# Attention and a bilinear GLU on one core: in the value products, the order of a head group's pieces

## Chip, core and metric

The kernel runs on one core of one Trainium2 chip. The metric is device time in microseconds (us) for one execution. Before the change it is 262.96 us, the median of 3 runs (262.53 to 263.45).

## The reference

One input x of 2048 rows and 512 columns is normalised and feeds two branches, and x and both branches are added. All tensors are bfloat16.

```
B, S, D = 1, 2048, 512;  H = 32; Dh = 16; W = 256;  F = 1792
xn = _layernorm(x)                                  # no scale, no shift
# branch A: attention in a sliding window
q, k, v = heads of (xn @ wqkv)                      # 32 heads of 16
scores = einsum("bhqd,bhkd->bhqk", q, k) * Dh**-0.5
mask = (i - j >= 0) & (i - j < W)                   # i: query, j: key
p = softmax(where(mask, scores, -1e9))
A = (einsum("bhqk,bhkd->bhqd", p, v), heads side by side) @ wo
# branch B: a GLU whose gate has no nonlinearity
g = xn @ w_gate;  u = xn @ w_up
Bout = (g * u) @ w_down
return x + A + Bout
```

## The kernel before

**Chunks and head groups.** The 2048 rows are worked in 4 chunks T of 512 queries. The 32 heads are handled as 4 head groups c of 8 heads: 128 of the 512 columns of q, which lie on the partitions as 4 row blocks of 32, each with an even and an odd head. A key tile is 128 columns of K: 64 keys for the even head and the same 64 for the odd one (two masks on K, line 284). In a chunk there are 8 such key tiles of its own (m = 0 to 7), and 4 of the chunk before are still inside the window (m = -4 to -1).

**Pieces.** With queries counted in blocks of 64, key tile m meets only its own block and the four behind it. A piece is (m, q0, q1): key tile m against query blocks q0 to q1. The constant `LATER` (line 21) lists the pieces of a head group of chunks 1 to 3 in five batches:

```
LATER = (((-2, 0, 2), (0, 0, 4)), ((5, 5, 7), (1, 1, 5)), ((-3, 0, 1), (7, 7, 7), (3, 3, 7)),
         ((-4, 0, 0), (6, 6, 7), (2, 2, 6)), ((-1, 0, 3), (4, 4, 7)))
```

In columns (64 per query block) that is 192, 320 | 192, 320 | 128, 64, 320 | 64, 128, 320 | 256, 256. A batch fills at most 512 columns, one PSUM bank for each of the four row blocks.

**Scores.** `scores` (line 361) multiplies a batch's pieces for the four row blocks (32x128 array tiles), and ScalarE (ACT) takes the exponential of all of it into a strip P (line 352). GpSimd (POOL) zeroes the far corner of the window (lines 181 and 354), VectorE (DVE) the near one (`mask_diag`, line 439). `strip` (line 325) notes each piece of a batch in `self.parts[T, c]`, in the order in which the strips are made.

**Value products.** `values` (line 451) is called once for each chunk and head group when its strips are masked. It goes through the noted pieces. For each piece there are 8 weight loads and 8 products, on 8 array tiles of 64 rows by 32 columns: two halves of the key tile (`par`: even and odd heads) and four row blocks (`e`). The weights are 32 columns of V, or of VS, which is V with its 64-row halves swapped; the moving operand is the piece's columns of P; the result is added in two PSUM banks `acc` (in the very last call `L`). The value tile carries columns of ones, so the softmax's sums come along. `start` is set on the first piece, `stop` on the last. Two transposes on VectorE (line 476) take the banks out; `divide` (line 480) divides and transposes once more. A head group of chunks 1 to 3 has 12 pieces, so 96 weight loads and 96 products; in chunk 0 it has 9 pieces.

**The order of all work is written out by hand.** `run` (line 630) goes through the batches as steps; between two steps it puts `fillers`: the projections, gate and up products (lines 499 and 510), each 128x512, on PE. `PAIRS` (line 27) says which head groups' values are taken in one go: in chunk 1 and 2 groups 0 and 1, then 2 and 3; in chunk 3 groups 0 and 1, then 2 alone, and 3 alone at the end. So chunks 1 to 3 have seven calls or pairs of calls, and chunk 0 four single ones.

**The down phase.** In chunks 1 to 3 seven batches, from the fourth of head group 0 to the last of head group 1, are taken in `down_phase` (line 398) together with the down products (line 532) of the chunk before. Three of them (the third, fourth and fifth of head group 1) are spread by row block over four steps, and their strips are made before those of the two batches in front of them. So in head group 1 the pieces are noted as 128, 64, 320 | 64, 128, 320 | 256, 256 | 192, 320 | 192, 320; in groups 0, 2 and 3 they stand as in `LATER`.

**Waits.** PE's instructions carry their semaphore waits themselves. The first product of a piece whose columns were masked waits for that mask.

Of the kernel before, what the change touches and what calls it, by code (L numbers as in the profile page):

```python
# [20 lines left out]
LATER = (((-2, 0, 2), (0, 0, 4)), ((5, 5, 7), (1, 1, 5)), ((-3, 0, 1), (7, 7, 7), (3, 3, 7)),  # L21
         ((-4, 0, 0), (6, 6, 7), (2, 2, 6)), ((-1, 0, 3), (4, 4, 7)))
REST = (((0, *SIX), (1, *SIX), (0, *FOUR)), ((1, *FOUR), (2, *FOUR)), ((2, *SIX), (3, *SIX), (3, *FOUR)))
SCORES, VALUES, SECOND = 1.9, 6.0, 5.0
FIRST = 3
GAP = 10.6
# [9 lines left out]
class Kernel:  # L36
# [279 lines left out]
    def batches(self, T):  # L316

        out = []
        for c in range(4):
            out += [tuple((c, *p) for p in pieces) for pieces in (LATER if T else SHARED)]  # L320
            if T == 0 and c < 3:
                out.append(REST[c])
        return out
# [127 lines left out]
    def values(self, T, c, accs=None):  # L451


        nc = self.nc
        if accs is None:
            accs = [self.m_tile([128, 512], F32, "acc") for _ in range(2)]
        todo = self.parts.pop((T, c))
        for i, (P, col, m, q, n) in enumerate(todo):
            U, j = divmod(8 * T + m, 8)
            b, h = divmod(j, 2)  # L460
            for par in range(2):
                rows = slice(64 * par, 64 * par + 64)
                for e in range(4):
                    if par == h:
                        at = 18 * (16 * (2 * b + par) + 4 * c + e)
                        v = self.V[U][rows, at:at + 32]
                    else:
                        at = 18 * (16 * b + 4 * c + e)
                        v = self.VS[U][rows, at:at + 32]
                    nc.tensor.matmul(accs[par][32 * e:32 * e + 32, q:q + n], lhsT=v,  # L470
                                     rhs=P[rows, e, col:col + n], start=(i == 0), stop=(i == len(todo) - 1),
                                     tile_position=(64 * par, 32 * e), skip_group_check=True)

        at = self.work.tile([128, 2, 16, 32], F32, tag="at", name="at")
        for par in range(2):
            nc.vector.transpose(out=at[:, par].rearrange("p b r -> p (b r)"), in_=accs[par][:])  # L476
        self.book("dve", TURN)
        self.at[(T, c)] = at
# [324 lines left out]
```

## Time and profile before

| | |
|---|---|
| median of 3 runs | 262.96 us (262.53 to 263.45) |
| the profiled execution | 262.99 us, its span 261.2 us |
| TensorE (PE) busy | 255.2 us, 98% of the span |
| ScalarE (ACT) busy | 183.4 us, 70% |
| VectorE (DVE) busy | 168.3 us, 64% |
| GpSimd (POOL) busy | 115.2 us, 44% |
| granted TensorE clock | 1.00 in every slice |

The span runs from the first to the last instruction of the program; the time holds what lies around it too (1.8 us here). "PE" are products, "PEld" weight loads, which overlap with them. In the profile's lines, a group of instructions has a line of the kernel, an engine, an operation and its operands with shapes; "xN" counts instructions. The line 470 holds the value products of all calls. The ends of products are modelled in such profiles, so a start is a better witness than an end. Times inside the span count from its start.

### The profile page before, as it was taken

What the parts mean: (1) busy time and instruction counts of PE and PEld (TensorE: products, weight loads), DVE (VectorE), ACT (ScalarE), POOL (GpSimd) and SP (SyncE); (2) the same over time, 40 slices, a digit from 0 to 9 for tenths busy, and PEclk for the clock granted to TensorE, in tenths of its full rate; (3) what the DMA queues carried; (4) which work ended last, traced back from release to release, by engine and by line L of the source; (5) the groups of instructions that cost most, each with busy time, mean ns of one, the idle gap of its engine ahead of it and who ended that gap; (6) DMA issues with size and microseconds to landing.
All of it is one profiled execution on the core that took longest, in us unless ns stands there. A gap on an engine that the chain in (4) does not pass through costs nothing.

```text
span 261.2 us, 7759 instructions
## 1 busy us (share of the span) xinstructions
PE 255.2 (98%) x3154; PEld 119.9 (46%) x3170; DVE 168.3 (64%) x342; ACT 183.4 (70%) x167; POOL 115.2 (44%) x278
## 2 busy tenths in 40 slices
PE   8999999999999999999999999999999999999995
PEld 7434444444444544444544454444544445434453
DVE  6777898888835488347976468641895235948144
ACT  3477778888586788787756768879874877877500
POOL 6226242425356745343445764334242565543500
PEclk9999999999999999999999999999999999999999
DMA  6999910120013230002001300000200100000002
GB/s 203 377 352 340 282 26 20 24 48 1 3 40 43 60 25 1 3 0 48 3 3 41 82 24 23 0 4 1 50 3 5 35 23 24 3 0 3 3 0 83
DMA packets 19426, 15.04 MB, mean 58 GB/s; under 512 B 7360, under 2 KB 19392, under 8 KB 19392
## 3 DMA queue, kind: packets, MB, share of 16 engines
q1 hardware_dynamic: 18848, 14.26, 19.8%
q8 instruction: 26, 0.43, 0.7%
q10 hardware_dynamic: 544, 0.30, 0.4%
q14 instruction: 8, 0.07, 0.1%
HBM read 9.70 MB, written 2.10 MB: 45 GB/s over the span
## 4 chain that ended last, share of the span: by engine, by line
PE 87%; DVE 8%; issue 2%; ACT 1%; DMA 1%; ACTq 1%
PE up L510 17%; PE gp L499 17%; PE psd L532 15%; PE qkp L274 9%; PE S L349 7%; PE acc L470 6%; PE vp L262 5%; PE psd L538 5%; PE L L532 2%; DVE at L476 2%; DVE hT L515 1%; DVE on L489 1%; PE B L349 1%; DMA x<-in_A_x_dram 1%; DVE st L192 1%
## 5 line engine op out<-in xcount | busy, mean ns | idle before, releaser
L181 POOL TENSOR_SCALAR_AFFINE_SELECT P<-P 64x256 bf16<-64x256 bf16 x224 | 99.2, 443 | 122.5 <-ACT P L352 108.0
L352 ACT ACTIVATE P<-S 128x2048 bf16<-128x2048 f32 x66 | 123.8, 1876 | 24.6 <-PE S L349 19.3
L499 PE MATMUL gp<-xnT,Wg 128*128 128x512 bf16 x224 | 59.1, 380 | 0.0
L510 PE MATMUL up<-xnT,Wu 128*128 128x512 bf16 x224 | 59.0, 380 | 0.0
L515 DVE TENSOR_TENSOR hT<-up,gsb 128x512 bf16<-128x512 f32 x56 | 37.9, 683 | 25.4 <-ACT gsb L253 13.1
L532 PE MATMUL psd<-Wd,hT 128*128 128x512 bf16 (+1 forms) x200 | 46.7, 368 | 0.8 <-issue 0.5
L447 DVE TENSOR_TENSOR P<-P,diag 128x512 bf16<-128x512 bf16 (+1 forms) x75 | 29.4, 392 | 16.0 <-ACT P L352 15.9
L253 ACT ACTIVATE gsb<-gp 128x512 bf16<-128x512 f32 x49 | 28.5, 596 | 9.6 <-PE gp L499 9.6
L532 PEld LDWEIGHTS <-hT 128*128 128x128 bf16 x238 | 21.6, 98 | 25.6 <-issue 3.3
L510 PEld LDWEIGHTS <-Wu 128*128 128x128 bf16 x224 | 20.6, 98 | 25.8 <-issue 2.9
L499 PEld LDWEIGHTS <-Wg 128*128 128x128 bf16 x224 | 20.5, 98 | 25.4 <-issue 2.9
L352 ACT ACTIVATE P<-B 128x1536 bf16<-128x1536 f32 (+2 forms) x18 | 17.8, 1022 | 17.8 <-PE B L349 10.9
L274 PE MATMUL qkp<-xnT,Wqkv 128*128 128x512 bf16 x128 | 29.8, 380 | 0.0
L349 PE MATMUL S<-Q,K 32*128 32x320 bf16 (+4 forms) x624 | 28.7, 255 | 0.4 <-ACT P L352 0.4
L349 PEld LDWEIGHTS <-K 32*128 32x128 bf16 x720 | 11.5, 92 | 27.8 <-issue 26.9
L548 DVE TENSOR_TENSOR x<-psd,x 128x512 bf16<-128x512 f32 (+1 forms) x15 | 9.9, 664 | 21.0 <-PE psd L538 21.0
L476 DVE STREAM_TRANSPOSE at<-acc 128x512 f32<-128x512 f32 x30 | 19.1, 687 | 4.7 <-PE acc L470 4.7
L274 PEld LDWEIGHTS <-Wqkv 128*128 128x128 bf16 x128 | 11.8, 98 | 14.7 <-issue 1.6
L470 PE MATMUL acc<-P,V 64*32 64x320 bf16 (+4 forms) x672 | 17.7, 253 | 0.0
L470 PE MATMUL acc<-P,VS 64*32 64x320 bf16 (+4 forms) x672 | 17.7, 253 | 0.0
L470 PEld LDWEIGHTS <-V 64*32 64x32 bf16 x720 | 15.3, 91 | 2.3 <-issue 2.1
L262 PE MATMUL vp<-Wqkv,xnT 128*128 128x512 bf16 x60 | 15.1, 380 | 0.2
(56 smaller groups left out, 190.3 us busy)
## 6 DMA issues: line engine op xcount, KB each, us to landing
out_dram<-x SPq DMA_DIRECT2D x15, 128.0 KB, 1.7
Wg<-in_B_w_gate_dram SPq DMA_DIRECT2D x2, 896.0 KB, 10.8
Wu<-in_B_w_up_dram SPq DMA_DIRECT2D x2, 896.0 KB, 12.9
Wd<-in_B_w_down_dram SPq DMA_DIRECT2D x1, 1792.0 KB, 17.2
Wqkv<-in_A_wqkv_dram SPq DMA_DIRECT2D x3, 512.0 KB, 5.6
x<-in_A_x_dram SPq DMA_DIRECT2D x2, 512.0 KB, 8.6
VS<-V SPq DMA_DIRECT2D x6, 144.0 KB, 2.6
x<-in_A_x_dram SPq DMA_DIRECT2D x3, 256.0 KB, 6.7
```

The source lines that it names most:

```text
L181: nc.gpsimd.affine_select(out=v, in_=v, pattern=pattern + [[1 if diag else -1, 64]], compare_op=ALU.is_ge if diag else ALU.is_gt, fill=0.0 ...
L253: nc.scalar.activation(out=out, in_=in_, func=ACT.Copy)
L262: nc.tensor.matmul(ps[:], lhsT=self.xnT[T][:, b, k, :], rhs=self.Wqkv[:, k, 1024:1536], start=(k == 0), stop=(k == 3))
L274: nc.tensor.matmul(ps[:], lhsT=self.Wqkv[:, k, lo:lo + 128], rhs=self.xnT[T][:, :, k, :], start=(k == 0), stop=(k == 3))
L349: self.nc.tensor.matmul(kw.pop("out"), start=True, stop=True, skip_group_check=True, **kw)
L352: self.nc.scalar.activation(out=out, in_=in_, func=ACT.Exp, scale=0.25)
L447: self.nc.vector.tensor_tensor(out=v, in0=v, op=ALU.min, in1=self.diag.unsqueeze(1).unsqueeze(1).to_broadcast([128, 4, n, 64]))
L470: nc.tensor.matmul(accs[par][32 * e:32 * e + 32, q:q + n], lhsT=v, rhs=P[rows, e, col:col + n], start=(i == 0), stop=(i == len(todo) - 1), ...
L499: nc.tensor.matmul(ps[:], lhsT=self.Wg[:, k, 128 * f:128 * f + 128], rhs=self.xnT[T][:, :, k, :], start=(k == 0), stop=(k == 3))
L510: nc.tensor.matmul(ps[:], lhsT=self.Wu[:, k, 128 * f:128 * f + 128], rhs=self.xnT[T][:, :, k, :], start=(k == 0), stop=(k == 3))
L515: nc.vector.tensor_tensor(out=self.hT[T, f][:], in0=ps[:], in1=self.gsb[:], op=ALU.mult)
L532: nc.tensor.matmul(ps, lhsT=self.hT[T, f][:, 128 * b:128 * b + 128], rhs=self.Wd[:, f, c0:c1], start=(f == 0), stop=False)
```

## The change

A constant lists the key tiles m in a new order, and `values` sorts a head group's pieces by it in chunks 1 to 3. Chunk 0 is left as it is.

```
+ORDER = (0, 1, 3, 2, -2, 5, 7, -3, -4, 6, -1, 4)
...
         todo = self.parts.pop((T, c))
+        if T:
+            todo.sort(key=lambda part: ORDER.index(part[2]))
         for i, (P, col, m, q, n) in enumerate(todo):
```

In columns the pieces then come as 320, 320, 320, 320, 192, 192, 64, 128, 64, 128, 256, 256, in all four head groups. In groups 0, 2 and 3 the last batch's two pieces of 256 columns stay last; in group 1, where they stood in the middle, they come last too. `start` moves to the piece of key tile 0, `stop` stays on, or moves to, that of key tile 4. The number of instructions is the same.

## The prediction

> **What bounds the kernel now.** I read the page's busy times first, then the chain of waits, then the windows of the value products (line 470), then single instructions of those windows.
>
> ```profile
> span 261.2 us, 7759 instructions
> ## 1 busy us (share of the span) xinstructions
> PE 255.2 (98%) x3154; PEld 119.9 (46%) x3170; DVE 168.3 (64%) x342; ACT 183.4 (70%) x167; POOL 115.2 (44%) x278
> ...
> PE 87%; DVE 8%; issue 2%; ACT 1%; DMA 1%; ACTq 1%
> ```
>
> TensorE (PE) is busy 98% of the span and carries 87% of the chain, so a nanosecond more or less in a run of its instructions is a nanosecond at the end, unless the chain leaves PE soon after. The chain of waits around the single call of head group 2 in chunk 3, and after the pair of groups 2 and 3 of chunk 1, shows both cases (start us, length us, what):
>
> ```profile
> 234.82 0.33 PE S L349 x8
> 235.15 1.28 PE acc L470 x94
> 236.43 0.75 PE gp L499 x3
> ```
>
> ```profile
> 123.47 1.26 PE acc L470 x93
> ...
> 124.75 2.51 DVE at L476 x4
> ...
> 133.33 1.26 DVE hT L515 x2
> ...
> 134.63 0.21 PE B L349
> ```
>
> In the first the whole call lies on the chain, in the second only the first head group of the pair: from there the chain runs through VectorE (DVE) to 134.6, where PE had stood about 0.16 us (its last product starts at 134.134, the next at 134.633; 0.216 of these 0.499 us are the product's own, about 0.127 such a switch costs on average). Chunk 2 does the same at 197.3.
>
> The changed calls, in windows from a call's first product to the next product behind it (stretch; length; PE busy with line 470, PEld likewise):
>
> ```profile
> 89.92:92.38 2.46, 2.45 (x192) 2.20 (x192) 1.00 0.04 10
> 123.40:125.80 2.40, 2.40 (x192) 2.15 (x192) 1.00 0.03 7
> ...
> 235.08:236.36 1.28, 1.28 (x96) 1.03 (x96) 1.00 0.06 13
> ```
>
> Calls of two groups take 2.45 us (groups 0 and 1, three times) or 2.40 (groups 2 and 3, twice), a single one 1.28 (twice): 14.7 us of 261 in all. That is the whole of what the change touches.
>
> Inside a call, a piece is 8 weight loads and 8 products on 8 array tiles at once, and on one tile a piece starts 136 ns (320 columns), 109 (256), 82 (192), 56 (128) or 29 (64) after the one before: columns at 2.4 per ns and 2 to 3 ns. Summed over the 12 pieces this is 1094 ns in any order; with 12 ns that the first piece of every call costs more (whether it has 64x128, 64x192 or 64x256: chunk 0 shows all three), 24 ns from tile 1 to tile 8 and 94 ns to the next product, 1224. The single call takes 1279: 55 are lost, and the trace shows where:
>
> ```profile
> 123.91 0.20 PE L470 MATMUL acc<-P,VS 64*32 64x64 bf16 x4
> ...
> 123.93 0.21 PEld L470 LDWEIGHTS <-V 64*32 64x32 bf16 x8
> 123.93 0.31 PE L470 MATMUL acc<-P,VS 64*32 64x320 bf16 x4
> 123.95 0.32 PE L470 MATMUL acc<-P,V 64*32 64x320 bf16 x8
> 124.06 0.11 PEld L470 LDWEIGHTS <-VS 64*32 64x32 bf16 x4
> 124.08 0.21 PE L470 MATMUL acc<-P,VS 64*32 64x64 bf16 x4
> ```
>
> (Instructions in order of time, merged; start, length.) Weight loads normally run a whole piece ahead of the products. Here, behind the pieces of 128 and 64, they stop. Number the instructions of a call from 0, sixteen to a piece: number 112, the first load of the eighth piece, starts 560 ns after the call's first product, number 114 only at 638. Sixty-four places before 114, the last product in front is number 49: it starts at 311 and lasts 296, so it ends at 607, 31 ns before. The same 31 ns stands at number 162 (859; product 97 ends at 828), at number 242 of the first call of chunk 1 (1321; product 177 ends at 1290) and at number 130 of chunk 0's third call (748; product 65 ends at 717). So I read: an instruction gets its place 31 ns after the products up to 64 places before it have ended, in order, and loads that come this way follow each other every 8.3 ns, not 3.3. A product of 320, 256, 192, 128, 64 columns lasts 296, 269, 243, 216, 189 ns, so it holds a place 327, 300, 274, 247, 220 ns: a short piece holds one nearly as long as a long piece. What costs is four pieces with few columns behind each other.
>
> **The change, part by part.** It removes and adds nothing: 96 loads and 96 products a group as before, the same transposes, no DMA, no queue passed. It sorts the pieces to 320, 320, 320, 320, 192, 192, 64, 128, 64, 128, 256, 256. Chunk 0 keeps its order.
>
> *The four long ones in front.* 4 x 136 ns; they change nothing by themselves, as the 12 ns of the first piece are there for any length.
>
> *The four small ones in a row.* Unhindered starts of a single call on tile 1: 0, 147, 283, 419, then 192s at 555 and 637, 64 at 719, 128 at 748, 64 at 804, 128 at 833, 256s at 889 and 998. With places: the second load of the second 64 waits for the first 192's first product, 555 + 274 = 829; the eighth comes 6 x 8.3 later, 879, its product at 883 instead of 828. The second 128's second load: 637 + 274 = 911, its eighth 961, product 965 instead of 857. Two loads on, 978, the first 256's second load; its eighth 1028, product 1032 instead of 913: 119 ns late, and the last piece stays so. The call ends at 1032 + 109 + 107 + 94 = 1342 against 1279: 63 more.
>
> *Second group of a pair.* It starts with its tiles already 58 ns apart, so the loads' pace costs less. Tile 8 of the second 128: its load waits 274 - 8 + 4 = 270 ns from the second 192, where columns ask 82 + 29 + 56 + 29 = 196: 74 late, plus 10 (66 instead of 56) at the 256: 84. Before, groups 2 and 3: 2400 - 1279 - 1094 = 27 late. So 57 more. Group 1 stands otherwise: its strips come out of the down phase in another order, so it began with 128, 64, 320, 64, 128, 320, and 2451 - 1279 - 1094 = 78 are lost. Its pair goes to 2400 + 63 + 57 = 2520: 69 more.
>
> *Sum.* Singles 2 x 63 = 126. Pairs of 0 and 1: 3 x 69 = 207. Pairs of 2 and 3: the first group's 63 pass down the DVE chain; the second's 57 fall into PE's 0.16 us at 134 and 197, and the DVE's third transpose, which starts about 0.12 us after that group's end, has room as well: 2 x 63 = 126. Together 0.46 us. If that cover is gone, 0.11 more.
>
> *What the rule misses.* In group 1 of the old order, the 128 behind the 64 comes 85 ns later where the rule gives about 33: 52 unexplained, the one row where a small cluster follows another closely. Bounds for the new cluster: 0 and 52 in each of 10 groups that count, 0 to 0.52 us. I take half, 0.26: the new cluster is denser than that row's, but follows a full queue. The other end, below nothing: if nothing stalls, what is lost now comes back, 7 x 55 + 3 x 78 = 0.62 us.
>
> [...]
>
> *Waits.* Group 1's second piece now comes from the strip made last. Its masks end at 89.00 (DVE) and 89.73 (POOL); the piece starts at about 91.2. Chunks 2 and 3 have at least as much as 1.4 us. The last batch, whose masks run until 90.67, stays last. No wait is added.
>
> The profiled execution took 262.99 us (span 261.2), 0.03 above the median 262.96. Forecast 262.96 + 0.46 + 0.26 = 263.7.
>
> **Rivals.** *Not slower: places come free early.* If a short product gave its place back sooner, so that the second 128's load waits under 196 ns from the 192's start instead of 274, nothing stalls and up to 0.62 comes back: 262.3. For it: the rule is read from products of 320 and 256 alone. Against: 31 ns four times. *No change:* the stalls come, but PE's waits behind them absorb them as at 134; then only some 0.1 us is left, 263.1. Against: behind five of the seven calls the chain stays on PE. *Much slower:* each of the four small pieces stalls by itself, as the 64 in group 1 did: 3 x 52 more in 10 groups over 0.46 is 1.6 beyond it, 265.0; half of it is 264.2. *Not as said* would be a chunk left unsorted; the sort covers every call with T over 0, so I give it nothing.
>
> **How the numbers follow.** A measurement of this kernel tells about 0.3%, 0.79 us, from no change. Forecast 0.72, own range 263.3 to 264.0 (bounds 0.46 and 0.98 and the spread of the runs); it straddles 263.75: 0.41 slower, 0.31 same. No change 0.08. Much slower 0.08. Not slower 0.12, of which 0.05 read as faster. Together slower 0.49, same 0.46, faster 0.05. With no change and the forecast 0.80 is held from 262.8 to 264.2; the runs' spread makes it 262.7 to 264.3.
>
> **What would show it.** Right: the single call near 235 grows from 1.28 to 1.34 us or more; all five pairs come to 2.52 or more; loads of the second 128 start about 0.91 us into the call; the products' forms keep their durations; PE starts its scores at 134.6 later by what the first group lost. Wrong: calls of 1.22 us, or a new wait of line 470 for POOL or DVE.

## The result, and the profile after

The changed kernel takes 263.42 us (median of 6 runs, 263.31 to 264.01), the kernel before 262.53 in the same comparison (6 runs, 262.48 to 263.45). The ratio is 1.003, with a 95% interval of 1.0019 to 1.0042: 0.79 us slower (0.50 to 1.10). The forecast was 263.7, within 262.7 to 264.3.

From here on, line 470 of before is line 473, and its lines 255, 274, 349 and 476 are 256, 275, 350 and 479. The page's span and busy times after:

```profile
span 261.5 us, 7761 instructions
...
PE 256.0 (98%) x3154; PEld 121.0 (46%) x3170; DVE 169.1 (65%) x342; ACT 183.5 (70%) x167; POOL 115.3 (44%) x278
```

PE is busy 0.8 us longer with the same 3154 recorded products. Where, the windows of the value products show (after; stretch from a call's first product to the next product behind it, its length, busy time of PE and PEld with line 473 alone, clock, DMA):

```profile
89.50:92.03 2.53, 2.53 (x192) 2.29 (x192) 1.00 0.03 9
123.06:125.60 2.54, 2.54 (x192) 2.30 (x192) 1.00 0.00 0
...
235.19:236.54 1.35, 1.35 (x96) 1.11 (x96) 1.00 0.00 0
```

By single instructions, all five pairs take 2.536 to 2.539 us now, whichever groups they hold: 86, 88 and 85 ns more for groups 0 and 1 (from 2.451 or 2.452), 139 and 136 more for groups 2 and 3 (from 2.399 and 2.401). The single call near 235 takes 1.349, 70 more, and the last one, whose next product is missing in both traces, is 68 longer up to the one after that. Together 0.67 us. The products of each form last as long as before within 4 ns (medians of 189, 223, 243, 273 and 296 ns for 64 to 320 columns, before 189, 220, 243, 269 and 297), and PE's clock is 1.00 in both. PE's loads of the short pieces of the call near 235, in order of time (after; start, length):

```profile
235.91 0.13 PEld L473 LDWEIGHTS <-VS 64*32 64x32 bf16 x4
235.96 0.16 PEld L473 LDWEIGHTS <-V 64*32 64x32 bf16 x8
236.04 0.11 PEld L473 LDWEIGHTS <-VS 64*32 64x32 bf16 x4
236.08 0.13 PEld L473 LDWEIGHTS <-V 64*32 64x32 bf16 x4
```

Four loads of one piece normally start within about 0.01 us and so show 0.10 here (each load lasts 0.09 to 0.10); groups of 0.13 and 0.16 are loads that wait for places one by one.

The chain of waits behind the first changed pair of groups 2 and 3 (after):

```profile
123.13 1.33 PE acc L473 x92
...
124.48 2.51 DVE at L479 x4
...
127.00 0.69 DVE Q L256
...
134.43 0.21 PE B L350
```

It has the same links as before. But PE's first score of this row now starts 11.37 us after the pair's first product, where it was 11.23: all 0.139 us by which the pair grew came through, not the first group's share alone.

### The profile page after: what moved, and what is told of

It is laid out like the page before. It is cut to its first block, busy times and chain, and to the rows that moved or that the text cites. A ratio compares the mean times of both kernels' runs of the same rounds, so it can differ in the third digit from the quotient of the medians.

```text
span 261.5 us, 7761 instructions
## 1 busy us (share of the span) xinstructions
PE 256.0 (98%) x3154; PEld 121.0 (46%) x3170; DVE 169.1 (65%) x342; ACT 183.5 (70%) x167; POOL 115.3 (44%) x278
## 4 chain that ended last, share of the span: by engine, by line
PE 90%; DVE 7%; issue 1%
PE up L513 17%; PE gp L502 17%; PE psd L535 15%; PE qkp L275 10%; PE S L350 8%; PE acc L473 6%; PE vp L263 5%; PE psd L541 5%; PE L L535 2%; PE wps L151 2%; DVE at L479 2%; DVE hT L518 1%; DVE on L492 1%; PE B L350 1%; PE L L541 1%
## 5 line engine op out<-in xcount | busy, mean ns | idle before, releaser
L448 DVE TENSOR_TENSOR P<-P,diag 128x512 bf16<-128x512 bf16 (+1 forms) x75 | 30.1, 401 | 16.1 <-ACT P L353 15.9
L473 PE MATMUL acc<-P,VS 64*32 64x320 bf16 (+4 forms) x672 | 18.5, 254 | 0.0
L473 PEld LDWEIGHTS <-VS 64*32 64x32 bf16 x720 | 15.8, 91 | 0.6 <-DMA x<-in_A_x_dram 0.2
```

Source lines behind the costliest of these rows:

```text
L448: self.nc.vector.tensor_tensor(out=v, in0=v, op=ALU.min, in1=self.diag.unsqueeze(1).unsqueeze(1).to_broadcast([128, 4, n, 64]))
```

## Experiments

The theory (A) is the prediction's: an instruction of PE gets its place when the products up to 64 places ahead have ended, so what costs is short pieces behind each other. The rivals B and C of the expectations put the loss on each short piece by itself (B), or on neighbours that add to the same columns (C). "Calls" below is the sum of the seven calls against before, from each kernel's own profile.

### The short pieces spread between long ones

```
-ORDER = (0, 1, 3, 2, -2, 5, 7, -3, -4, 6, -1, 4)
+ORDER = (0, 7, 1, -3, 3, -4, 2, 6, -2, 5, -1, 4)
```

In columns 320, 64, 320, 128, 320, 64, 320, 128, 192, 192, 256, 256.

> All 12 pieces of every head group of chunks 1 to 3, in the order 320, 64, 320, 128, 320, 64, 320, 128, 192, 192, 256, 256 columns: no two short pieces side by side. Theory A (an instruction gets its place 31 ns after the products up to 64 places before it have ended): any four neighbours ask for at least 357 ns where a place is held 332 at most, so hardly anything stalls. Single call 1.23 us (before 1.28, changed 1.35), pairs 2.33 (2.40 and 2.45; 2.54). Seven calls together 0.67 us under before, 261.8 to 262.0 where before reads 262.5; ratio 0.9975. Rival B (a short piece costs about 66 ns for its 16 instructions, wherever it stands): as before or up to 0.1 us above. Rival C (pieces that add to the same columns of a bank one after the other stall): the short ones here follow a long one that covers their columns, so a call is slower than before.

Measured: 262.08 us against 262.75, ratio 0.9981 (0.997 to 0.9992). Two pairs and a single call of this kernel, windows as above:

```profile
123.00:125.34 2.34, 2.33 (x192) 2.12 (x192) 1.00 0.03 7
186.00:188.48 2.48, 2.47 (x192) 2.16 (x192) 1.00 0.00 0
234.44:235.68 1.24, 1.24 (x96) 1.04 (x96) 1.00 0.00 0
```

To the next product it is 2.328 to 2.330 for four pairs and 1.231 and 1.233 for the singles, and on the first tile the pieces follow by their columns alone: 136, 28 to 29, 136 to 137, 55 to 56, 82 to 83, 109 ns. The two pieces of 128 and the second 64, which took 67 to 83 ns in the changed order, take their columns' 28 to 56 here. That is A, and against B. Against C it says less than the expectation has it, as the pieces of 64 share no columns with the long piece in front of them. But in the changed order the four 320s share most of their columns and still follow every 135 to 136 ns (147 behind the call's first). Calls: 0.47 us less, though two losses of another kind stand against it. One is in the pair at 186.0, 0.139 us long. The other is behind the first call of chunk 1, in the chain of waits of this kernel:

```profile
93.16 0.43 PE up L513 x2
93.60 0.02 issue
93.62 0.59 PE up L513 x2
```

In the middle of four equal up products PE stands: the third should start 0.216 us after the second, and starts 0.19 later than that. No semaphore ends this; the spread order with moved instruction blocks, further below, returns to it.

### The short pieces first

```
+ORDER = (7, -3, -4, 6, 0, 1, 3, 2, -2, 5, -1, 4)
```

> The changed kernel's run of four short pieces (64, 128, 64, 128) moved to the front of the group, the rest in its order. Theory A: the 64 places are all free at the start of a call, so the four short ones run at their columns' pace and only the fifth piece's loads wait, for the first piece's products (220 ns after they start, where columns ask 181): single call 1.29 to 1.30 us, pair about 2.48 since the second group meets a full queue. Time 0.3 us over before (after is 0.8 over). Rival B (66 ns for each short piece) and rival C (same neighbours, same columns): as the changed kernel, 1.35 and 2.54, 0.8 us over before.

Measured: 263.28 us against 262.75, ratio 1.002 (1.0011 to 1.0028). Single calls 1.310 and 1.312, less than the changed order's 1.349: with an empty queue in front, the cluster costs less. The second 64 adds to columns of the 128 just in front of it, and the two follow each other at their columns' pace (57 and 28 ns), which is against C. The fifth piece's second load waits for the first 64: that product lasts 199 ns, 10 more than a later one as it is the call's first, and the load comes at 230, 31 ns after its end. So a short product does not return its place early. The pairs, 2.551 to 2.553, missed the expectation by 0.07. Their second group begins behind the first one's two pieces of 256, which still hold their places (an instruction behind a 256 waits 300 ns), so the cluster there starves as it does in the changed order: its pieces follow after 28, 57, 101 and 130 ns. I had taken the state of the queue at the second group wrongly; the rule itself explains the miss.

### The pieces of 192 ahead of all

```
+ORDER = (-2, 5, 0, 1, 3, 2, 7, -3, -4, 6, -1, 4)
```

The cluster stays the same, but 320s instead of 192s stand right before it.

> The changed order with the two pieces of 192 moved to the front: 192, 192, 320, 320, 320, 320, 64, 128, 64, 128, 256, 256. The same run of short pieces meets other pieces four places back. Theory A: the second 64 waits for the place of a 320 four pieces back, which ends early enough (332 against 357), so it starts 85 ns after the first 64 (104 in the changed kernel); the second 128 waits for a 320 (332 against 250) and starts 167 ns after the first 64 or later (186 there). Single call 1.35 us. A price of 66 ns for each short piece gives the changed kernel's 104 and 186, since the four short ones and their number are the same.

Measured: one run, 263.18 us; pairs 2.538 and 2.539, singles 1.348 and 1.350, the same as in the changed order within 3 ns. Inside the call the second 64 starts 85 ns behind the first, where A has it; a fixed price for each short piece would have left it at the changed order's 104. The second 128 starts at 905, 187 behind the first 64 (changed order 186), which does not tell A and B apart by itself. But its second load starts at 909. Sixty-four places ahead, the fourth 320's first product started at 583 and lasts 296: it ends at 879, and 879 + 31 = 910.

### The listed order in group 1 alone

```
+ORDER = (-2, 0, 5, 1, -3, 7, 3, -4, 6, 2, -1, 4)
...
+        if T:
+            todo.sort(key=lambda part: ORDER.index(part[2]))
```

Everything else is as before; only group 1, where the strips come in another order, is put into the order of `LATER`.

> Head group 1 of chunks 1 to 3 takes its pieces in the order of LATER, as the other groups do; nothing else differs from before. If the 52 ns that its call loses over the other pairs' come from the order, the three pairs of groups 0 and 1 go from 2.45 to 2.40 us and the kernel is 0.15 us faster, ratio 0.9994. If they come from the place (down phase just ended, what lies around), the pairs stay at 2.45 and the time stays.

Measured: 262.75 us against 262.75, ratio 1.0001 (0.9992 to 1.001), which can't resolve the 0.15. But the calls can: the three pairs of groups 0 and 1 take 2.402 to 2.403, from 2.451 and 2.452, and so match those of groups 2 and 3. The 52 ns that the prediction could not explain belong to the order of group 1 and to nothing else about its strips. Why the rule misses them in that order stays open. (In this profile one pair of groups 2 and 3 took 2.632, with a stop of 0.23 us in it, and PE stood 0.29 us at 94.1: the same kind of stop as in the first experiment.)

### The new order in group 3 of chunks 1 and 2 alone

```
-        if T:
+        if T in (1, 2) and c == 3:
```

This is the second group of the two pairs whose growth the prediction had covered.

> The changed order in head group 3 of chunks 1 and 2 alone, the second group of the pairs at 123 and 187 us; all else as before. The prediction's reading (VectorE has room behind the first group, PE stands 0.16 us before the down phase): the pair grows to about 2.47 and the scores of the down phase at 134.6 keep their distance from the pair's first product. The other reading (VectorE's next instruction, the copy of Q, waits for a projection that PE does behind the pair): the distance grows by the 65 ns, and the end by 0.13 us.

Measured: one run, 263.01 us; the time of a single run says little, the trace more. VectorE in the pair at 123.17 (in order of time; start, length; last the idle time before, and its releaser):

```profile
124.53 2.51 DVE L479 STREAM_TRANSPOSE at<-acc 128x512 f32<-128x512 f32 x4 [0.28 <-PE acc L473]
127.05 0.69 DVE L256 CAST Q<-qkp 128x512 bf16<-128x512 f32 x1
```

The pairs took 2.468 and 2.470, 69 ns more. The transposes start as in before, 1.351 us after the pair's first product, so the DVE's own row of work is not late. Yet its copy of Q comes 3.872 after the pair's first product, 3.803 in before, and the first score of the next row 0.070 and 0.074 us later than in before. What moved is the projection that Q is copied from. Projection and copy in before, whose pair starts at 123.40:

```profile
126.13 1.04 PE L274 MATMUL qkp<-xnT,Wqkv 128*128 128x512 bf16 x4
127.20 0.69 DVE L255 CAST Q<-qkp 128x512 bf16<-128x512 f32 x1
```

The projection here, and from the chain of waits the first score of the next row:

```profile
125.97 1.04 PE L275 MATMUL qkp<-xnT,Wqkv 128*128 128x512 bf16 x4
134.48 0.21 PE B L350
```

PE does the projection behind the pair; it ends at 3.835 here, 3.765 before and 3.905 in the changed kernel, and Q starts 37 or 38 ns after it in all three (times from the pair's first product). The trace names the transpose as Q's predecessor, since that also ends at this point, but only the projection moved.

### The spread order, with the instruction blocks moved

```
-PADS = {27: 120, 47: 178}
+PADS = {5: 200, 27: 176, 47: 178}
```

`PADS` gives the number of empty instructions on PE, put between fillers, at a step of the row of batches. They shift all later instructions in the blocks in which PE's program is loaded (see the last section). The order is that of the first experiment.

> The first experiment's order (no short pieces side by side) and 200 nops on PE, three behind each filler from step 5 on, with those at step 27 raised from 120 to 176, so that PE's instructions reach the call of groups 0 and 1 of chunk 1 at another place of their 256-instruction blocks, the place that the same calls of chunks 2 and 3 have. In the first experiment PE stood 0.19 us behind that call, in the middle of an up product's four, 1.41 us after the end of an instruction block's transfer. If that is a block that comes too late, the stop goes away, and the time is 0.2 us under the first experiment's: 261.8 where before reads 262.6 (ratio 0.997). If the stop is a wait of another kind (a bank, VectorE), it stays and so does the ratio of 0.998. If 256 more instructions on PE cost time by themselves, it is above that.

Measured: 262.02 us against 262.72, ratio 0.9971 (0.9959 to 0.9982), the fastest kernel here, some 0.6% below the changed one by their two ratios. All five pairs take 2.328 to 2.330, both singles 1.232, and nothing stands at 93.6. Calls: 0.61 us less.

The same pads on the kernel before:

```
-PADS = {27: 120, 47: 178}
+PADS = {5: 200, 27: 176, 47: 178}
```

> The nops of the run beside it, in the old order. There the same block came in time by a hair (one weight load 0.16 us late, no product late), so the time stays as before: ratio 0.999 to 1.001. If it moves by more, the nops do something else, and the other run's gain is theirs in part.

Measured: 262.99 us against 262.72, ratio 1.001 (1.0001 to 1.0019). The calls are unchanged to 2 ns; the pads cost 0.19 us, all of it in one place at 43.3 us. So they bring nothing by themselves: the gain is the order's, and what the pads add is that two stops are gone. That the intervals of the two spread kernels overlap leaves the size of it open.

### Empty instructions inside a group

```
+            if T and i == 4:
+                for _ in range(32):
+                    nc.tensor.nop("pad", nofuse=True)
```

Before's order, with 32 empty instructions ahead of the fifth piece of each group in chunks 1 to 3, to see whether they take places too.

> The old order with 32 nops on PE ahead of the fifth piece of every head group of chunks 1 to 3. If a nop takes one of the 64 places, the 320 behind the first short ones finds only half of them for products: its loads wait for those of the piece two in front instead of four, and a single call takes 1.40 us or more instead of 1.28. If nops take no place and only their 4 ns each, 133 ns fall beside the two pieces in front (218 ns), and a call takes 1.28 to 1.33.

Measured: one run, 296.73 us, which neither reading expected. The page's PEclk row, and PE in the single call near 265 (in order of time):

```profile
PEclk9999999999997799997999979999699997999999
```

```profile
265.07 0.31 PE L473 MATMUL acc<-P,V 64*32 64x320 bf16 x4
267.25 0.24 PE L473 MATMUL acc<-P,VS 64*32 64x128 bf16 x4 [1.87 <-issue]
```

The fifth piece starts 2.19 us after the fourth instead of 0.136, with "issue" as the reason: about 64 ns for each empty instruction. The queue runs dry during that time, so the kernel says nothing about places. The expectation's 4 ns for each is half of the 8.3 ns at which loads come; the empty instructions that before itself has (298, from `PADS`) start at least 70 ns apart in its trace.

## Why the prediction was right, and where it was not

**The rule of places** held. In all traces but that of the last experiment, none of the 8352 loads of these calls that have 64 instructions in front starts sooner than 30 ns after the products up to 64 places ahead have ended; counted by 62 places, 1021 start sooner than that. As loads and products alternate, 64 places for both can't be told from 32 for products alone. In the call near 235 the second 64's eighth product starts at 881 (883 worked out), the second 128's second load at 909 (911, the first case behind a product of 192), its eighth at 959 (961) and its product at 964 (965), the first 256's eighth product at 1030 (1032). The call takes 1349, not 1342. The excess comes behind the cluster: the first 256's loads still come every 8.3 ns while it runs, and the last 256 gets its eighth product at 1147 where the sum assumed 1032 + 109 = 1141.

**Second group of a pair.** It is 1189 ns behind the first (2538 - 1349), 95 more than its columns; 84 was worked out. Pairs of groups 0 and 1 reach 2.538 instead of 2.520 for these two reasons: both groups are 7 to 11 ns undersized.

**The cover** is the step that failed: "the second's 57 fall into PE's 0.16 us at 134 and 197, and the DVE's third transpose ... has room as well". The room in the transposes was there; the next thing on VectorE was not looked at. The copy of Q needs PE's projection, which stands behind the pair, and it starts 37 to 38 ns after the projection's end already in before. So nothing is covered. The group 3 kernel shows it, with the transposes where they were and the score 70 and 74 ns later. "If that cover is gone, 0.11 more" stood in the text; it was 0.14 (2 x 69). (PE's stand at 134 was nearer 0.19 us than 0.16: the switch from a 512-column product to scores takes 95 or 96 ns in 58 of before's 61 cases.)

**The sum.** Worked out 0.46 (0.126 singles, 0.207 pairs of 0 and 1, 0.126 pairs of 2 and 3). Measured in the calls: 0.138, 0.259 and 0.275, 0.67 in all. The reserve of 0.26 for "what the rule misses" was given to a stall like that of the old group 1. No such stall appeared, and the listed order in group 1 shows that it went with the order that was removed. The forecast of 0.72 was right in size because this reserve stood in for the missing cover and the sizes; that part was luck.

**Where the rest lies.** In the two profiled executions the stretch from the first changed call to the end is 0.69 us longer, and the calls hold 0.67 of it; all that lies between and behind them differs by 0.02. The executions as a whole differ by only 0.32 us (262.99 and 263.31), as that of before stood 0.43 us later at its first changed call, by a delay in the first 17 us; its other runs lie mostly at 262.5. The ratio of the runs gives 0.79 and their medians 0.89. What these have over 0.69 can't be placed: it is less than what the runs of one kernel differ by.

**The rivals.** *Places come free early* would have shown calls near 1.22: wrong here. The spread order comes to 1.23 with places that are held as long as before. *Each small piece by itself* is wrong by the spread order. The Trainium skill ("TensorE: Matmul & The Clock Gate", "Back-to-back issue gap") gives N / 2.4 + 2.5 ns as the gap of an isolated product, and says that in a stream of loads and products it comes out too small for small N. Here, with eight tiles in use, the pieces of the spread order follow by it within 1 ns for all five sizes; in the cluster a 64 takes up to 54 ns more. *No change* had PE's waits absorb the stalls; the chain shows none of that.

## What to carry to other kernels

In a run of small products the order is worth time at equal work: a place in PE's queue is held for nearly as long by a short product as by a long one (here 220 ns at 64 columns, 327 at 320), so mix short pieces among long ones, until a piece and the three behind it bring clearly more column time than its place is held. In the spread order the four from any 320 on bring 356 or 357 ns against 327; in the changed order the four from the second 192 on bring 196 against 274. At 96 products a group either way, the changed order loses 0.67 us on the order before, and the spread order gains 0.47 to 0.61. When work is called covered by another engine's room, follow that engine past its next step too, and ask which of its inputs come from the delayed engine.

## What was not expected of the hardware

**Empty instructions are not free on PE.** 32 of them added 2.05 us to one single call and 1.99 to the other, some 62 to 64 ns each. Of the 256 that the pads added to before's order, nearly all cost nothing, as they stand between products of 512 columns. What they cost, 0.19 us, is lost at 43.3 us: there six of them stand 71 ns apart right behind chunk 0's second call of value products, and PE waits for the load behind them. In the run with 32 in each head group PE's clock fell: 0.6 to 0.7 in some slices, 0.959 on average.

**Late instruction blocks.** The page lists 26 transfers of kind "instruction" on one queue, 0.43 MB: 16 KB each, and at 256 instructions apiece room for 6656, about what PE has (3154 products, 3170 loads, the empty ones). The two kernels with 256 more empty instructions have 27. The stop at 93.62 ends 1.41 us after the end of such a transfer (91.248 + 0.958). In the group 1 kernel the stop ends at 94.15, 1.41 after its transfer; in before a load at 94.17 stands as close behind its own, but early enough for its product. The stops inside a pair (the first experiment's at 186.0 and that of the group 1 kernel) end 1.34 and 1.39 us after theirs. In the first experiment the two stops begin at PE's instructions 2242 and 4802, exactly 10 blocks of 256 apart. They cost 0.14 to 0.29 us each. The Trainium skill ("Runtime: NRT & Kernel Launch", "Instruction fetch mechanics") says that programs come in blocks of 256 and that crossing into the next is mostly hidden; the size agrees, and at these spots it was not hidden. That the block is the cause was not tested by itself: in the spread kernel with pads the stops are gone, which is what it predicts, at one place of the pads.

**Products of different tiles start out of order.** In before's pair at 123.4, a product of the 320 behind a 64 starts 1649 ns into the call, the 64's last one at 1680. On one tile they keep the order.
